# Part B of a two-part kernel: output of 32 tokens on four column tiles, the 8 look-ahead rows multiplied at the end

## Chip, cores and metric

One core of one Trainium2 chip. The metric is the device time of one execution in microseconds, the median of the runs (lower is better).

## What is computed

The output is two independent blocks joined along the last axis. Part A is a dilated sliding-window attention over 2048 tokens of width 640; the change leaves its instructions alone. Part B is a recurrent-memory transformer layer:

```
S, Dm, H, Dh, M, seg_len = 2048, 640, 32, 192, 8, 32          # 64 segments
mask = (idx[:, None] < M) | (idx[:, None] >= idx[None, :])     # over L = 40 tokens
for s in range(n_seg):
    h = concatenate([mem, x[32*s : 32*s+32]])                  # 8 memory + 32 tokens
    q, k, v = h @ Wq, h @ Wk, h @ Wv                           # each 40 x (32 heads x 192)
    p = softmax(where(mask, q k^T * Dh**-0.5, -1e9))
    o = (p v).reshape(40, 6144) @ Wo                           # 40 x 640
    mem = o[:8]                                                # goes into the next segment
    outs.append(o[8:])
```

All inputs and the output are bf16. The memory rows make the 64 segments a chain. Wq, Wk and Wv are 640 x 6144 and Wo is 6144 x 640, some 31 MB in all, which is more than fits on the core beside the rest.

## The kernel before, in words

**Weights.** Part B cuts each of Wq, Wk, Wv into 4 head groups g of 1536 columns and 5 pieces of 128 input rows (`dc`), and Wo into 24 units i of 256 rows. Such a unit is one [128, 1536] or [128, 1280] bf16 block (384 or 320 KB). Most stay on the core ("resident", tiles `wres_*`); 24 of them are fetched again in every segment through a ring of six buffers (`wstream`, tag `ws`, line 417, printed as `t<-wcopy_*`): 2 in each k group, 2, 2, 1 and 1 in the v groups, and the Wo units of `STREAMED["o"]`. SyncE issues these fetches in program order, and a fetch waits until TensorE has used the unit that was in its buffer six fetches before. Before Part B starts, the streamed units are copied into contiguous DRAM blocks (`wcopy_*`), and x is copied into one window per segment (`xwindows`, line 382).

**Tokens on the narrow side.** A projection (`project32`, line 485) takes 32 tokens as the stationary operand: four matmuls, one for each of TensorE's four 32-column tiles, each with 384 weight columns as the moving operand. A window holds two sets of 32 tokens. `main(s)` is the 8 memory rows and the first 24 tokens of segment s. `ahead(s)` is the last 8 tokens ("late rows") of four consecutive segments; these don't depend on the memory, so they are projected once for four segments (`RENEW`) and kept in buffers `Lb` (q, k) and `LV` (v). A DMA transpose (line 469) lays the window of the next segment out as [128 input rows, 5, 64].

**One segment**, the function `segment`, whose order on TensorE is written by hand: for each group g the projections of q, k, v; a turn of q and k by matmuls with the identity (line 498) into `QT` and `KT`; `scores` (line 575, 16 matmuls of 64 output rows); `softmax` and `put_p` on VectorE (lines 582 to 600) with the exponential on ScalarE (line 588); `turn_p` (lines 610 and 613); `mix` (line 627: 32 matmuls with 32 rows of weights and 40 columns on four row tiles, into four PSUM tiles, copied to `OT` by ScalarE and VectorE in turn, line 465). The groups are interleaved, so that TensorE works on another group while one is in its softmax. `project_out` (line 641) adds, over all 24 Wo units, the product of `OT` with Wo into one PSUM tile `Y` [128, 320]: 40 of 64 stationary columns are tokens, and two column tiles hold the two halves of the 640 output columns. For every segment it runs in six stretches, of 6, 4, 2, 4, 2 and 6 units.

**The boundary between segments.** When the last unit is in `Y`, ScalarE copies it to SBUF (line 708), TensorE turns the 8 memory rows with the identity (`memory_rows`, line 654, after four filler matmuls, line 648), and VectorE writes them into the next window `HX` (line 657). Only then can the next segment's first projection start. To have work at that point, TensorE projects one q group of late rows (`ql`) in two parts, three pieces ahead of the last Wo units and two behind.

**Engines.** The order on TensorE is fixed by hand; on the others a scheduler sets it. PSUM has 8 buffers of one bank in Part B: three `acc`, four `x` (turns, scores, mix) and one `y`. GpSimd copies kept late rows into `QT` and `KT` and issues the output DMAs.

Of the kernel before, what the change touches and what calls it, by code (L numbers as in the profile page):

```python
# [23 lines left out]
def part_a(ctx, tc, A_x, A_wqkv, A_wo, out, ident, emit_loads):  # L24
# [239 lines left out]
    with tc.manual_schedule(engines={mybir.EngineType.PE, mybir.EngineType.DVE, mybir.EngineType.Activation}):  # L264
# [4 lines left out]
        for b in range(-1, n_blk):  # L269
# [13 lines left out]
STREAMED = {"k": ((2, 4), (2, 4), (0, 4), (0, 4)), "v": ((0, 4), (0, 4), (2,), (2,)),  # L283
            "o": (3, 5, 7, 10, 11, 13, 17, 18, 22, 23)}
# [3 lines left out]
LEAD_IN, PAD = 114, 4  # L288
# [9 lines left out]
def part_b(ctx, tc, B_x, B_mem0, B_Wq, B_Wk, B_Wv, B_Wo, out, ident, n_seg, pre, nbuf, mid):  # L298
# [6 lines left out]
    w_in = {m: w.rearrange("(dc p) h e -> p dc (h e)", p=128) for m, w in (("q", B_Wq), ("k", B_Wk), ("v", B_Wv))}  # L305
    wo_v = B_Wo.rearrange("h e d -> (h e) d").rearrange("(i k p) d -> p i k d", p=128, k=2)

    def unit_src(u):  # L310
        m, c, dc = u
        if m == "o":
            return wo_v[:, c]
        return w_in[m][:, dc, 1536 * c:1536 * c + 1536]

    def unit_cols(u):
        return 1280 if u[0] == "o" else 1536

    copied = {}

    def copy_streamed():

        order = [(m, g) for m, g in need]
        units = []
        for m, g in order:
            if m == "o":
                units += [("o", i, 0) for i in range(6 * g, 6 * g + 6) if i in STREAMED["o"]]
            else:
                units += [(m, g, dc) for dc in range(5) if m != "q" and dc in STREAMED[m][g]]
        for u in units:  # L330
            copied[u] = dpool.tile([128, unit_cols(u)], BF16, name="wcopy_%s%d_%d" % u)[:]
            nc.sync.dma_start(unit_tile(copied[u], u), unit_src(u))
# [4 lines left out]
    for m, g in need:  # L337
        if m == "o":
            resident += [("o", i, 0) for i in range(6 * g, 6 * g + 6) if i not in STREAMED["o"]]
        else:  # L340
            resident += [(m, g, dc) for dc in range(5) if m == "q" or dc not in STREAMED[m][g]]
    res, wait = {}, set()

    def unit_tile(t, u):
        v = t[:, 0:unit_cols(u)]
        return v.rearrange("p (k d) -> p k d", k=2) if u[0] == "o" else v

    def place_resident(pool, units):
        for u in units:
            res[u] = pool.tile([128, unit_cols(u)], BF16, name="wres_%s%d_%d" % u)[:]  # L350

    def load_resident(units, engs):
        for k, u in enumerate(units):
            engs[k % len(engs)].dma_start(unit_tile(res[u], u), unit_src(u))
# [8 lines left out]
    XW = dpool.tile([n_seg, 2 * SEG, Dm], BF16, name="xwindows")  # L363

    def copy_windows():

        rows = [(XW[0, 0:M], mem2[0:M]), (XW[0, M:SEG], x2[0:SEG - M])]
        for a, b in ((1, 49), (49, n_seg)):
            rows.append((XW[a:b, 0:SEG], x2[SEG * a - M:SEG * b - M].rearrange("(s n) d -> s n d", n=SEG)))
        groups = x2.rearrange("(t n) d -> t n d", n=SEG)[:, SEG - M:SEG]  # L370
        groups = groups.rearrange("(m k) n d -> k m n d", k=4)
        windows = XW[:].rearrange("(m k) n d -> k m n d", k=4)
        for r in range(4):
            for i in range(4):
                dst = windows[r][:, SEG + M * i:SEG + M * i + M]
                if i >= r:
                    rows.append((dst, groups[i]))
                else:
                    rows.append((dst[0:n_seg // 4 - 1], groups[i][1:n_seg // 4]))
                    rows.append((dst[n_seg // 4 - 1], groups[i][n_seg // 4 - 1]))  # L380
        for dst, src in rows:
            nc.sync.dma_start(dst, src)

    def emit_loads(turn_x):
        turn_x(1)
        load_resident(resident[:n_pre], [nc.sync])
        turn_x(2)
        copy_streamed()
        return copy_windows
# [7 lines left out]
    HXs = [xpool.tile([128, 5, 64], BF16, name=f"HX{i}") for i in range(2)]  # L397
# [5 lines left out]
    qk_sb = pool("b_qk", bufs=3)  # L403
# [7 lines left out]
    wait.update(resident[n_pre + len(early):])  # L411
# [8 lines left out]
    def get_unit(u):  # L420
        if u in fetched:
            return fetched.pop(u)
        if u in res:
            if u in wait:
                wait.remove(u)
                load_resident([u], [nc.sync])
            return res[u]
        return fetch(u)
# [11 lines left out]
    KT = cpool.tile([128, 4, 4, L], BF16, name="KT")  # L440
# [3 lines left out]
    OT = cpool.tile([128, 12 * L + PADW], BF16, name="OT")  # L444
    free = [cpool.tile([128, 3, 4, M], BF16, name=f"Lb{i}") for i in range(BLOCKS)]
    late = {}
    VW = 448
# [3 lines left out]
    nc.gpsimd.memset(KT[:], 0.0)  # L451
    for t in [QT, OT]:
        nc.gpsimd.memset(t[:, t.shape[1] - PADW:], 0.0)
    for t in LV + [Vst]:
        nc.gpsimd.memset(t[:, 192:256], 0.0)

    copies = {"n": 0}
    S_, V_ = nc.scalar.copy, nc.vector.tensor_copy
    ENGINES = {"sb": {"q": (V_, S_, S_, S_), "k": (S_, S_, S_, S_)}, "late": (V_, V_, V_, V_),
               "QT": (S_, S_, S_, V_), "KT": (S_, S_, S_, S_), "V": (S_, V_, V_, S_), "LV": (V_, S_, S_, V_),  # L460
               "PT": (S_, V_, V_, V_)}

    def evacuate(dst, src):
        copies["n"] += 1
        (S_ if copies["n"] % 2 else V_)(dst, src)  # L465

    def load_x(s):
        if s < n_seg:
            nc.sync.dma_start_transpose(HXs[s % 2][:], XW[s])

    def main(s):
        return HXs[s % 2][:, :, 0:SEG]

    def ahead(s):
        return HXs[s % 2][:, :, SEG:2 * SEG]

    def project32(Xs, m, g, dcs=range(5), ps=None):
# [3 lines left out]
        for dc in dcs:  # L481
            w = get_unit((m, g, dc))
            for n, X in enumerate(Xs):
                for j in range(4):
                    nc.tensor.matmul(ps[n][32 * j:32 * j + 32, :], lhsT=X[:, dc, :],  # L485
                                     rhs=w[:, 384 * j:384 * j + 384],
                                     start=(dc == 0), stop=(dc == 4), tile_position=(0, 32 * j))
# [7 lines left out]
    def turn(sb, chunks=(0, 1, 2)):  # L495
        pt = ps_x.tile([128, len(chunks), 4, 32], FP32, tag="x", name="pt")
        for k, c in enumerate(chunks):
            nc.tensor.matmul(pt[:, k], lhsT=sb[:, 128 * c:128 * c + 128], rhs=ident, start=True, stop=True)  # L498
        return pt

    def tokens(t):
        return t[:, 0:12 * L].rearrange("p (j c n) -> p j c n", c=3, n=L)

    def fill(copy, m, n0, n1, src):

        if m == "q":
            copy(tokens(QT)[:, :, :, n0:n1].rearrange("p j c n -> p c j n"), src)  # L507
            return
        fill_outer(copy, n0, n1, src[:, 0:3:2])
        fill_middle(copy, n0, n1, src[:, 1])  # L510

    def fill_outer(copy, n0, n1, src):
        copy(KT[:, :, 0:3:2, n0:n1].rearrange("p j c n -> p c j n"), src)  # L513

    def fill_middle(copy, n0, n1, src):
        copy(KT[0:64, :, 1, n0:n1], src[0:64])
        copy(KT[64:128, :, 3, n0:n1], src[64:128])  # L517

    def turn_late(sb, m, g, s, start):

        pt = turn(sb)
        for t in range(start, next_start(m, g, start)):
            rows = pt[:, :, :, M * (t % 4):M * (t % 4) + M]
            if t == s:
                if m == "k" and g == 0:
                    fill_middle(V_, 32, L, rows[:, 1])
                    fill_outer(S_, 32, L, rows[:, 0:3:2])
                else:
                    fill(S_, m, 32, L, rows)
# [266 lines left out]
```

## Time and profile before

| what | us |
|---|---|
| median of three runs | 1973.57 |
| lowest and highest run | 1972.08, 1983.03 |
| span of the profiled execution, first to last instruction | 1976.8 |
| first projection of Part B | 171.1 |
| last Wo matmul starts after | 1969.9 |
| copies of the memory rows into HX, the first and the last | 218.36, 1943.46 |

The page gives no device time of the profiled execution beside its span. The profile has, for each engine, its busy time; a TensorE row's busy time is a union of overlapping matmuls. "DMA share" is the mean busy share of the core's 16 DMA engines. The chain of waits follows the work that ended last backwards: it names at each time what the program was waiting for. A releaser behind "<-" is what ended an idle time.

### The profile page before, as it was taken

To read this page: it belongs to the slowest core of one execution; us is meant where nothing else is said; L and a number is where in the kernel's file an instruction comes from. 1 tells how busy PE (TensorE), PEld (TensorE's weight loads), DVE (VectorE), ACT (ScalarE), POOL (GpSimd) and SP (SyncE) were. 2 spreads that over 40 slices of the span, in tenths; PEclk is the share of its full clock that TensorE was granted. 3 is DMA by queue.
4 is the path that set the end of the run, shared out by engine and by line. 5 is a ranking of instruction groups with operands and counts; after the bars stand their busy time and mean duration, and the time that the engine had idled before them with its cause. 6 is when DMAs were issued, how large, how long until landed. Compare 5 with 4: busy or idle time off the path is not lost.

```text
span 1976.8 us, 99618 instructions
## 1 busy us (share of the span) xinstructions
PE 1890.8 (96%) x43006; PEld 1221.6 (62%) x43006; DVE 1032.1 (52%) x3431; ACT 927.4 (47%) x2963; POOL 262.3 (13%) x1070
## 2 busy tenths in 40 slices
PE   8998899999999999999999999999999999999998
PEld 5665566666666666666666666666666666666665
DVE  4885454455444554455445554455445554555454
ACT  3554344444444454444444454444444444444443
POOL 2001011111111111111111111111111111111111
PEclk9999999999999999999999999999999999999999
DMA  9936999999999999999999999999999999999997
GB/s 332 298 111 227 341 324 312 327 326 326 324 321 324 322 328 315 329 319 331 326 318 322 329 330 314 325 315 316 327 328 324 327 327 315 338 325 329 315 328 262
DMA packets 278203, 621.62 MB, mean 314 GB/s; under 512 B 62089, under 2 KB 72329, under 8 KB 277449
## 3 DMA queue, kind: packets, MB, share of 16 engines
q1 hardware_dynamic: 272258, 609.17, 91.3%
q8 instruction: 337, 5.52, 1.1%
q0 software_dynamic: 5504, 6.07, 1.0%
q14 instruction: 104, 0.85, 0.1%
HBM read 602.01 MB, written 19.27 MB: 314 GB/s over the span
## 4 chain that ended last, share of the span: by engine, by line
PE 67%; DMA 17%; ACT 7%; DVE 6%; issue 2%; SPq 0%; ACTq 0%; POOL 0%; POOLq 0%; DVEq 0%
PE acc L485 31%; PE Y L641 17%; DMA t<-wcopy_k 7%; PE pt L498 7%; DMA t<-wcopy_o 6%; DMA t<-wcopy_v 4%; PE Sps L575 3%; PE pq L95 3%; PE OTps L627 3%; DVE prod L151 1%; ACT sb L712 1%; ACT OT L708 1%; PE pt L610 1%; ACT KT L513 1%; ACT t L588 1%
## 5 line engine op out<-in xcount | busy, mean ns | idle before, releaser
L485 PEld LDWEIGHTS <-HX 128*32 128x32 bf16 x19380 | 467.1, 96 | 283.8 <-issue 54.5
L641 PEld LDWEIGHTS <-OT 128*64 128x64 bf16 x6144 | 317.8, 110 | 137.0 <-ACT OT L465 25.0
L485 PE MATMUL acc<-t,HX 128*32 128x384 bf16 x4524 | 342.9, 328 | 19.0 <-DMA t<-wcopy_k 9.3
L641 PE MATMUL Y<-wres_o,OT 128*64 128x320 bf16 x3584 | 331.2, 302 | 9.9 <-DVE OT L465 5.1
L485 PE MATMUL acc<-wres_q,HX 128*32 128x384 bf16 x6460 | 333.6, 328 | 1.1 <-issue 0.7
L492 ACT CAST sb<-acc 128x384 bf16<-128x384 f32 x448 | 210.1, 478 | 152.0 <-PE acc L485 132.4
L641 PE MATMUL Y<-t,OT 128*64 128x320 bf16 x2560 | 266.7, 301 | 10.4 <-DMA t<-wcopy_o 8.8
L485 PE MATMUL acc<-wres_v,HX 128*32 128x384 bf16 x4520 | 251.7, 327 | 0.7 <-DMA wres_v<-in_B_Wv_dram 0.7
L485 PE MATMUL acc<-wres_k,HX 128*32 128x384 bf16 x3876 | 224.6, 327 | 0.3 <-DVE sb L492 0.3
L588 ACT ACTIVATE t<-t 128x160 f32<-128x160 f32 x256 | 86.4, 338 | 288.5 <-DVE t L587 284.5
L498 PE MATMUL pt<-ident,sb 128*128 128x128 bf16 x1938 | 182.4, 221 | 8.5 <-ACT KT L513 0.9
L582 DVE SCALAR_TENSOR_TENSOR t<-Sps,mask 128x160 f32<-128x160 f32 x256 | 82.9, 324 | 178.5 <-PE Sps L575 173.2
L465 ACT CAST OT<-OTps 128x120 bf16<-128x120 f32 x512 | 108.6, 266 | 140.4 <-PE OTps L627 139.2
L498 PEld LDWEIGHTS <-sb 128*128 128x128 bf16 x1938 | 109.4, 97 | 87.0 <-ACT sb L492 20.5
L590 DVE TENSOR_REDUCE sm<-t 128x4 f32<-128x160 f32 x256 | 82.0, 320 | 130.9 <-ACT t L588 130.9
L465 DVE CAST OT<-OTps 128x120 bf16<-128x120 f32 x512 | 123.7, 272 | 46.1 <-PE OTps L627 45.8
L513 ACT CAST KT<-pt 128x256 bf16<-128x256 f32 (+1 forms) x323 | 109.1, 343 | 78.6 <-PE pt L498 78.1
L517 POOL COPY KT<-Lb 64x32 bf16<-64x32 bf16 x189 | 40.0, 212 | 788.2 <-PE Sps L575 656.9
L575 PEld LDWEIGHTS <-QT 128*64 128x64 bf16 x4096 | 98.4, 112 | 59.1 <-issue 52.2
L575 PE MATMUL Sps<-KT,QT 128*64 128x40 bf16 x4096 | 113.9, 187 | 5.6 <-ACT QT L507 2.6
L657 DVE CAST HX<-pt 128x40 bf16<-128x40 f32 x63 | 12.6, 200 | 179.5 <-PE pt L654 179.5
L600 DVE TENSOR_TENSOR P<-t,sm 128x128 bf16<-128x128 f32 (+1 forms) x512 | 100.2, 237 | 11.2
(91 smaller groups left out, 2130.8 us busy)
## 6 DMA issues: line engine op xcount, KB each, us to landing
t<-wcopy_o SPq DMA_DIRECT2D x640, 320.0 KB, 4.9
t<-wcopy_k SPq DMA_DIRECT2D x512, 384.0 KB, 5.3
t<-wcopy_v SPq DMA_DIRECT2D x384, 384.0 KB, 5.3
wres_q<-in_B_Wq_dram SPq DMA_DIRECT2D x20, 384.0 KB, 7.8
wres_v<-in_B_Wv_dram SPq DMA_DIRECT2D x14, 384.0 KB, 7.9
wres_k<-in_B_Wk_dram SPq DMA_DIRECT2D x12, 384.0 KB, 7.8
wres_o<-in_B_Wo_dram SPq DMA_DIRECT2D x14, 320.0 KB, 7.1
wcopy_o<-in_B_Wo_dram SPq DMA_DIRECT2D x10, 320.0 KB, 9.6
```

The lines of the kernel that those rows point to most:

```text
L95: nc.tensor.matmul(pq[32 * d:32 * d + 32], lhsT=wcol[:, k, t, 4 * c + d, :], rhs=xTs[s][:, k, :], start=(k == 0), stop=(k == 4), tile_posi ...
L465: (S_ if copies["n"] % 2 else V_)(dst, src)
L485: nc.tensor.matmul(ps[n][32 * j:32 * j + 32, :], lhsT=X[:, dc, :], rhs=w[:, 384 * j:384 * j + 384], start=(dc == 0), stop=(dc == 4), tile_ ...
L492: copy(sb[:], p[:])
L498: nc.tensor.matmul(pt[:, k], lhsT=sb[:, 128 * c:128 * c + 128], rhs=ident, start=True, stop=True)
L513: copy(KT[:, :, 0:3:2, n0:n1].rearrange("p j c n -> p c j n"), src)
L575: nc.tensor.matmul(Sps[64 * g2:64 * g2 + 64, a, :], lhsT=QT[:, at:at + 64], rhs=KT[:, a, ((0, 1), (3, 2))[g2][part], :], start=(n == 0), s ...
L582: nc.vector.scalar_tensor_tensor(out=t1[:], in0=Sps[:], scalar=scale, in1=mask[:].unsqueeze(1).to_broadcast([128, 4, L]), op0=ALU.mult, op ...
L588: nc.scalar.activation(t1[:], t1[:], ACTF.Exp)
L590: nc.vector.tensor_reduce(out=sm[:], in_=t1[:], axis=AX.X, op=ALU.add)
L600: nc.vector.tensor_tensor(out=P[:, k, :, at:at + hi - lo], in0=t1[:, :, lo:hi], in1=sm[:].unsqueeze(2).to_broadcast([128, 4, hi - lo]), op ...
L641: nc.tensor.matmul(Y[64 * gv:64 * gv + 64, :], lhsT=OT[:, L * c:L * c + 64], rhs=w[:, n:n + 320], start=(i == 0 and r == 0), stop=(i == 23 ...
```

## The change

The diff rewrites much of Part B. It does this:

- **Output of 32 tokens.** `project_out` takes only the 32 `main` tokens: four matmuls per Wo unit (2 row halves r x 2 column halves gv), each on a 32-column tile of its own. Even and odd halves are added afterwards: `close` has ScalarE copy the odd half (2 copies of 64 x 160), VectorE add it to the even half (2 adds), transpose the sum in 32 x 32 blocks and copy 8 columns of each block into the next window.
- **Late rows at the end.** The mixed late rows of each segment are copied by GpSimd into a tile `OL` and written to DRAM (`late_o`, 96 KB per segment). After the last segment `project_late` reads them back (16 DMAs of 384 KB) and multiplies 512 rows by all of Wo, in two passes over the 24 units.
- **x turned by VectorE.** The window is loaded by a plain DMA (`XS`) and transposed in 32 x 32 blocks by VectorE (`turn_x`, in `segment` after `mix(2)`). For that the rows of Wq, Wk and Wv are regrouped, and the window copies in DRAM are cut into four parts of 160 columns (100 or so DMAs in place of 26).
- **Mix on 64-row tiles.** A mask `own` blanks foreign heads, so that `mix` is 16 matmuls with 64 rows and 80 columns, into two PSUM tiles; the copy of the turned P becomes a VectorE multiplication of 128 x 320 for every group.
- **Scores** work on a new layout of `QT` and `KT`: 8 matmuls with 64 rows and 8 with 128.
- **One engine for each PSUM tile**: all copies of one tile are on one engine, and `QT`/`KT` are filled by one copy. `memory_rows` and its fillers are gone; `ql` is split two and three; `tq` and `tk` turns stand at other places.

```diff
+    XW = dpool.tile([n_seg, 4, SEG, 2, 160], BF16, name="xwindows")
+    late_o = dpool.tile([n_seg, 128, 48 * M], BF16, name="late_o")
...
+    def load_x(s):
+        if s < n_seg:
+            nc.sync.dma_start(XS[:], XW[s].rearrange("j n w c -> (j n) (w c)"))
+    def turn_x(s):
+        if s < n_seg:
+            nc.vector.transpose(HXs[s % 2][:].rearrange("p w k n -> p (w k n)"), XS[:])
...
     def scores(g):
-        for n in range(8):
-            a, part = n // 2, n % 2
-            for g2 in range(2):
-                at = L * (3 * a + g2 + part)
-                nc.tensor.matmul(Sps[64 * g2:64 * g2 + 64, a, :], lhsT=QT[:, at:at + 64], ...
+        for outer in range(2):
+            for a in range(4):
+                for h in range(2):
+                    k0, k1, c = (0, 128, 2 * h) if outer else (64 * h, 64 * h + 64, 1)
+                    at = L * (4 * c + a)
+                    nc.tensor.matmul(Sps[64 * h:64 * h + 64, a, :], lhsT=QT[k0:k1, at:at + 64], ...
+                                     tile_position=(k0, 64 * h))
...
     def turn_p(g):
-        ENGINES["PT"][g](PT[:], pt[:].rearrange("p l (h n) -> p l h n", h=2)[:, :, :, 0:L])
+        nc.vector.tensor_tensor(PT[:], pt...to_broadcast([128, 4, 2, L]), own[:]...to_broadcast([128, 4, 2, L]), op=ALU.mult)
     def mix(g, PT):
+        plan = [(late, h, 0) for late in range(2) for h in range(2)] + [(late, h, 1) for late in range(2) for h in range(2)]
+        for n, (late, h, middle) in enumerate(plan):
+            k, col, lo, hi = (1, 128 + 64 * h, 64 * h, 64 * h + 64) if middle else (2 * h, 256 * h, 0, 128)
+            for r in range(2):
+                nc.tensor.matmul(ps[r][lo:hi, 2 * L * k:2 * L * k + 2 * L], lhsT=V[64 * r:64 * r + 64, col:col + hi - lo], ...
+        for r, copy in ((0, S_), (1, V_)):
+            copy(OT[:, 6 * r:6 * r + 6].rearrange("p c n -> p (c n)"), ps[r][:, 0:6 * L])
+        nc.gpsimd.tensor_copy(OL[:, :, 12 * g:12 * g + 12].rearrange("p n c -> p c n"), OT[:, :, 32:L])
...
     def project_out(Y, g, pairs=range(6)):
-                    nc.tensor.matmul(Y[64 * gv:64 * gv + 64, :], lhsT=OT[:, L * c:L * c + 64],
-                                     rhs=w[:, n:n + 320], ..., tile_position=(0, 64 * gv))
+                    t = 32 * (2 * r + gv)
+                    nc.tensor.matmul(Y[t:t + 32].rearrange("p (b c) -> p b c", b=2),
+                                     lhsT=OT[:, slot(c), 0:32], rhs=wide(w, r, gv),
+                                     start=(i == 0), stop=(i == 23), tile_position=(0, t))
+    def close(s, Y):
+        for b in range(2):
+            S_(odd[64 * b:64 * b + 64], Y[64:128, 160 * b:160 * b + 160])
+        for b in range(2):
+            nc.vector.tensor_tensor(Ysb[64 * b:64 * b + 64], Y[0:64, 160 * b:160 * b + 160],
+                                    odd[64 * b:64 * b + 64], op=ALU.add)
+        if s + 1 < n_seg:
+            nc.vector.transpose(T, Ysb)
+            nc.vector.tensor_copy(HXs[(s + 1) % 2][:, 0, :, 0:M], T.rearrange("p (k n) -> p k n", n=SEG)[:, :, 0:M])
+        for j in range(4):
+            nc.gpsimd.dma_start(out2[SEG * s:SEG * s + SEG - M, Dm + 160 * j:Dm + 160 * j + 160], Ysb[32 * j + M:32 * j + SEG])
+        nc.gpsimd.dma_start(late_o[s], OL[:].rearrange("p n c -> p (n c)"))
...
     def segment(s):
         mix(2, PT[2])
+        turn_x(s + 1)
         values(s, 3)
...
-            ql = project32([ahead(s + 1)], "q", gl, range(0, 3))
+            ql = project32([ahead(s + 1)], "q", gl, slice(0, 2))
         project_out(Y, 3)
-        nc.scalar.copy(Ysb, Y[:])
+        close(s, Y)
         if not last:
-            project32([ahead(s + 1)], "q", gl, range(3, 5), ql)
+            project32([ahead(s + 1)], "q", gl, slice(2, 5), ql)
             nc.scalar.copy(sb[:], ql[0][:])
-            memory_rows(s, Ysb)
-            turn_late(sb, "q", gl, s, s + 1)
+            turn_late(sb, "q", gl, s, s + 1, V_)()
+    def project_late():
+        for b in range(16):
+            nc.sync.dma_start(t, late_o[4 * b:4 * b + 4].rearrange("i p c -> p i c"))
+        for part in ((0, 1, 2), (3,)):
+            for i in range(24):
+                w = get_unit(("o", i, 0))
+                for r in range(2):
+                    for m in part:
+                        for gv in range(2):
+                            for j in range(4):
+                                nc.tensor.matmul(sums[2 * m + gv][32 * j:32 * j + 32, 0:320], lhsT=O[4 * m + j][:, :, at],
+                                                 rhs=w[:, 640 * r + 320 * gv:640 * r + 320 * gv + 320], ...)
+            for m in part:
+                ...  # two copies to SBUF, then 16 DMAs of 8 rows to the output, on SP and ACT in turn
```

349 lines of the change are left out of this document (179 added, 170 removed).

## The prediction

> **What bounds the kernel now.** I read the page first, then windows of a few microseconds, the waits of TensorE, the chain of waits through two segments, and the instruction orders of both programs.
>
> ```profile
> span 1976.8 us, 99618 instructions
> PE 1890.8 (96%) x43006; PEld 1221.6 (62%) x43006; DVE 1032.1 (52%) x3431; ACT 927.4 (47%) x2963; POOL 262.3 (13%) x1070
> q1 hardware_dynamic: 272258, 609.17, 91.3%
> ```
>
> TensorE is busy 96% of the span, but the DMA queue is at 91.3%: two resources are near their limits together. Windows tell how near the second one is:
>
> ```profile
> core 0: us, PE busy (x) PEld busy (x) DVE busy (x) ACT busy (x) POOL busy (x), PEclk, DMA share, GB/s
> 40.00:45.00 5.00, 5.00 (x92) 3.16 (x85) 4.20 (x5) 2.69 (x5) 0.00 (x0) 1.00 1.04 403
> 246.00:1943.00 1697.00, 1643.54 (x38938) 1063.46 (x38932) 863.60 (x3142) 802.63 (x2655) 231.21 (x976) 1.00 0.96 324
> ```
>
> With a deep queue of weight loads the DMA engines moved 403 GB/s; in Part B they move 324 at a share of 0.96. So the share overstates the load, and there is room for some 20% more. TensorE's waits for streamed units in this stretch are 8.6 + 6.8 + 5.9 = 21.3 us, 0.34 us in each of 62 segments.
>
> The copies of the memory rows stand at 218.36 and 1943.46, so a segment takes 1725.1 / 62 = 27.82 us. The chain through one segment without DMA waits (27.1 us), where a number behind x counts matmuls:
>
> ```profile
> 1027.80 2.55 PE acc L485 x60
> ...
> 1030.79 0.93 PE acc L485 x20
> 1031.72 0.02 issue
> 1031.74 0.43 PE Sps L575 x16
> ...
> 1037.73 0.31 PE OTps L627 x32
> ...
> 1039.52 1.75 PE Y L641 x24
> 1041.27 0.24 PE Sps L575 x16
> ...
> 1050.61 0.35 issue
> ...
> 1051.78 1.77 PE Y L641 x24
> 1053.55 0.03 ACTq L708
> 1053.58 0.04 issue
> 1053.62 0.43 ACT OT L708
> 1054.05 0.47 ACT sb L712
> 1054.51 0.05 issue
> 1054.56 0.34 PE pt L498 x3
> 1054.90 2.55 PE acc L485 x60
> ```
>
> It is TensorE nearly throughout. Sixty projection matmuls take 2.55 and twenty 0.93: 0.81 for twenty, so 0.162 for a set of four on four tiles, and 0.12 to enter. Scores take 0.43 behind a projection (32-column tiles) and 0.24 behind the output (64-column tiles, as their own): another form of tile costs 0.1 to 0.2.
>
> **Per segment, part by part.**
>
> *Output.* Now 96 matmuls at 1.75/24: 7.0. Afterwards 24 sets of four with 320 columns in place of 384: 0.162 x 320/384 = 0.135, so 3.25, and an entry of 0.12 in four of the six stretches (two now follow a projection and keep its form): 3.7. **-3.3**. That four tiles run side by side is what the projections show.
>
> *Boundary.* Now 1.35 from the end of Y (1053.55) to the next projection (1054.90). Afterwards ScalarE makes two copies of 64 x 160; its 64 x 128 copy takes 0.26 and its 128 x 320 one 0.43, so 0.29 each. Then come `sb` 0.47, hop 0.05, the turn 0.34, and VectorE's first copy of a late block (`Lb`, 0.26): in the built order it stands between the transpose and the copy into HX (0.2 in the old row), so the memory rows wait behind a turn that they don't need. With 0.07 and two short hops: 2.0. VectorE's own part (first add after 0.36, two adds at 0.35, a transpose) ends at 1.3 to 1.5 and is hidden by the turn. No row here has a VectorE transpose; its bounds are the 128 x 32 copy (0.17) and the 128 x 384 one (0.55), and for the 128 x 320 transpose of x I take 0.42, near the 128 x 320 copy. +0.65, less 0.16 for the third `ql` piece that now lies inside: **+0.5**. The output DMAs and `late_o` are on GpSimd (five at 0.5) ahead of its fills of QT and KT, which are needed only some 4 us into the segment: nothing.
>
> *Mix.* 32 matmuls of 40 columns take 0.31. Afterwards there are eight steps of 80 columns and, inside, a change from 64 x 128 to 64 x 64 tiles: at least 0.31, at most 0.5; I take 0.42, in the middle, since halves can overlap. **+0.45** for four (0 to +0.75).
>
> *Scores and turns.* The two score runs behind the output lose their cheap entry (0.2 and 0.1), each run changes its form inside (0 to 0.12; I take 0.05), and turns that stood in runs of six now stand alone (six in 0.44, three in 0.27: 0.1 twice): **+0.7**.
>
> [...]
>
> *Group 3.* From its scores to P takes 2.6 (three VectorE steps 0.32 to 0.35, exponential 0.34, sum 0.32, reciprocal 0.17, two products 0.47, one OT copy between). TensorE's cover is two Wo units, mix, v, four units: now 3.0 or so, afterwards 0.37 + 0.42 + 0.93 + 0.54 = 2.3. It waits 0.3 (not where v3 is renewed). Behind P, VectorE has the x transpose (0.42) and the wider PT (320 elements: 0.55 for 384, 0.33 for 160, so 0.49 in place of 0.33) before `mix(3)` may start; TensorE has two units: 0.4 of waiting, in place of the 0.35 at 1050.61 (not in each segment). **+0.4**.
>
> *Group 1.* PT of group 0 moves from ScalarE into VectorE's chain (0.49), and the built order puts an OT copy (0.41) ahead of the P products in three of four segments: P(1) is ready 6.3 after the first scores, TensorE at 5.7, unless a renewed k or v fills it. 0.6 in half of the segments: **+0.3**.
>
> *Waits for DMA.* Per segment 8.78 MB of units, and 0.2 of windows, late rows and output: 9.0 MB in 27 us is 333 GB/s. Against that, a window's DMA now holds SyncE 0.3 and not 1.2. I take +0.1, between -0.3 and +0.5.
>
> Sum: -3.3 + 0.5 + 0.45 + 0.7 + 0.4 + 0.3 + 0.1 = **-0.85**, a period of 27.0. VectorE's load rises from 13.7 to some 17 us, still two thirds. 63 segments: **-54 us**. The first one is bound by loads and stays.
>
> **The end.** From the last Y to the end now: 1970.6 to 1976.8, 6.2. Afterwards the first row of `project_late` needs twelve blocks of late rows; SyncE reaches eight of them only behind the last fetches, some 4.6 before the end of Y, and at 1.0 to 1.1 each (0.384 MB) they are in at +8. Pass one is 24 x 2 x 3 x 2 = 288 sets of four: 39. Pass two is 96 sets: 13, and 3 of waiting, since SyncE issues 24 output DMAs (0.3 to 0.5 each) ahead of its last fetches. Two copies, eight DMAs per queue and a landing: 7. Together 70, less 6.2 and rounding: **+65** (55 to 95).
>
> **The start.** SyncE issues 26 window DMAs from 92.84 to 116.17, 0.62 apart where nothing holds it; it then has slack to 146.9. Afterwards there are 104 with more, shorter rows: 104 x 0.62 = 64, and some 4 more in each part for the two long ones (estimate from the 2.5 of the first transpose with its thousands of rows): 173, and 3.5 for landing and turning, against 171.1: **+5** (0 to +35).
>
> 1976.8 - 54 + 65 + 5 = 1992.8. The span is 3.2 above the median of the runs: **1990**. Break-even is a period of 27.82 - 70/63 = 26.7.
>
> **Rivals.**
>
> *The waits don't come (faster).* Form changes cost nothing inside scores and mix (-0.9), and TensorE's early arrivals at P(3), mix(3) and P(1) are covered, since other stalls are gone with the single copies and the two free `x` buffers (-0.5): a period of 25.6, 1976.8 - 140 + 70 - 3 = 1904. It decides from 26.7 down. For it: ScalarE and VectorE copies in turn on one tile held each other up (VectorE 72.5 us, ScalarE 52.6 us behind each other's Lb copies). Against: the form change is seen in the rows, the VectorE order in the built program. 0.33.
>
> *DMA is the bound.* Its queue moved 609.17 MB in 91.3% of 1976.8: 337 GB/s while busy, and 9.0 MB at that rate is 26.7, to which the boundary's idle adds: 27.6. 1976.8 - 14 + 70 - 3 = 2030. Against: 403 GB/s with a deep queue. 0.13.
>
> *Start and end dearer.* [...] 0.09.
>
> *The four tiles don't overlap*, the output stays at 7: 27.82 + 2.5, and the late pass doubles: 2250. The projections speak against it. 0.03.
>
> My forecast, a period of 26.7 to 27.3 (1970 to 2010): 0.42.
>
> **Chances.** Runs of this kernel differ by about 0.5%, 9.9 us: 1963.7 to 1983.4 is the same. The forecast gives 0.11 same and 0.31 slower; the first rival 0.32 faster and 0.01 same; the forecast's lower edge adds 0.01 to faster, the others are slower. Faster 0.33, same 0.12, slower 0.55. The range 1920 to 2050 leaves out the fastest tenth (a period under 25.8) and the last rival.
>
> **What would show it.** Y sets at 0.135; 2.0 us between Y and the next projection, ending in HX behind an Lb copy; TensorE waiting at P(3) and mix(3) for PT; 65 to 70 us behind the last segment. A period under 26.7 makes it wrong; so does a DMA rate that stays at 324 while TensorE waits for `t`.

## The result, and the profile after

The changed kernel takes 2098.18 us (median of four runs, 2095.58 to 2111.01) against 1978.24 for the old one beside it: 1.062 times as long (95% interval 1.058 to 1.066). The forecast was 1990 with a range of 1920 to 2050. It was wrong. Here and below a time is the median of a kernel's executions, without those more than 1.5% above its fastest (two, of the kernel with half of the output, at a clock of 0.94 against 0.96 in its fastest).

The page of the changed kernel, in the same three lines as before:

```profile
span 2096.8 us, 92560 instructions
PE 1845.2 (88%) x39688; PEld 1105.1 (53%) x39688; DVE 1127.7 (54%) x3463; ACT 808.6 (39%) x2100; POOL 466.8 (22%) x1138
q1 hardware_dynamic: 287812, 622.35, 88.3%
```

TensorE is busy for 46 us less, in a span that is 120 us longer. The copies of the memory rows into HX (line 675) place these 120 us. The first one stands at 262.06 (before 218.36), the last at 1991.50 (before 1943.46). So the start costs +43.7; 62 periods of 27.89 in place of 27.82 cost +4.3; and what follows the last copy takes 105.3 in place of 33.3, +72.0.

Windows of the changed kernel: the loading of resident weights, the stretch behind it, and the middle of Part B (columns: busy time and instructions of each engine, then granted clock, DMA share, GB/s):

```profile
20.00:60.00 40.00, 37.34 (x596) 23.79 (x588) 29.79 (x31) 21.31 (x41) 0.00 (x0) 1.00 1.04 218
60.00:86.00 26.00, 0.01 (x3) 0.00 (x0) 0.00 (x0) 0.43 (x1) 0.00 (x0) 0.60 1.08 233
300.00:1850.00 1550.00, 1400.96 (x31285) 818.78 (x31285) 869.94 (x2895) 627.01 (x1669) 387.61 (x945) 0.99 0.94 326
```

The old kernel's window from 20 to 60 us:

```profile
20.00:60.00 40.00, 37.45 (x612) 24.55 (x604) 30.53 (x31) 21.62 (x40) 0.00 (x0) 1.00 1.09 368
```

From 20 to 60 us DMA now moves 218 GB/s, where it moved 368. From 60 to 86 us TensorE stands still, for the third transposed block of Part A's x lands behind these loads (one wait of 26.9 us). In Part B TensorE is busy 1401 of 1550 us (before 1502), and DMA moves 326 GB/s, as before.

The chain through a segment of the changed kernel:

```profile
1065.96 5.46 DMA t<-wcopy_o
...
1071.46 0.34 PE Y L660 x4
...
1071.87 0.29 ACT odd L668
...
1072.17 0.30 ACT odd L668
...
1072.90 0.33 DVE OT L670
...
1073.25 0.35 DVE T L674
1073.59 0.14 DVE Lb L551
1073.73 0.09 DVE HX L675
...
1073.87 1.81 PE acc L521 x40
...
1078.08 0.47 PE px L588 x16
...
1084.20 0.45 PE px L636 x16
...
1086.14 0.93 PE Y L660 x24
...
1087.28 6.66 DMA t<-wcopy_o
```

Fetches of units stand in the chain for 5 to 7 us at a time: the walk goes from TensorE to the fetch it waits for, and then to the earlier use that freed the fetch's buffer. They are not new, but they have grown: from 300 to 1940 us they are 28.0% of the chain (Wo 21.0, k 5.2, v 1.8), where the old kernel has 16.9% (Wo 6.3, k 6.9, v 3.7). New is the boundary: from the last Y (end 1071.80) to the projection (1073.87) it is ScalarE's two copies, VectorE's adds, transpose and two copies, 2.07 us in all.

### The profile page after: what moved, and what is told of

Its sections match the earlier page's. It is cut to its first block, busy times and chain, and to the rows that moved or that the text cites. A ratio compares the mean times of both kernels' runs of the same rounds, so it can differ in the third digit from the quotient of the medians.

```text
span 2096.8 us, 92560 instructions
## 1 busy us (share of the span) xinstructions
PE 1845.2 (88%) x39688; PEld 1105.1 (53%) x39688; DVE 1127.7 (54%) x3463; ACT 808.6 (39%) x2100; POOL 466.8 (22%) x1138
## 4 chain that ended last, share of the span: by engine, by line
PE 53%; DMA 31%; DVE 5%; SPq 4%; ACT 3%; issue 3%; ACTq 0%; DVEq 0%; POOLq 0%; POOL 0%
PE acc L521 29%; DMA t<-wcopy_o 19%; PE Y L660 6%; PE px L534 6%; DMA t<-wcopy_k 5%; PE px L588 4%; SPq L409 4%; PE px L636 3%; ACT odd L668 2%; DMA t<-wcopy_v 1%; PE px L756 1%; DVE OT L670 1%; DMA wres_k<-in_B_Wk_dram 1%; DMA wres_v<-in_B_Wv_dram 1%; DMA wres_q<-in_B_Wq_dram 1%
## 5 line engine op out<-in xcount | busy, mean ns | idle before, releaser
L642 POOL COPY OL<-OT 128x96 bf16<-128x96 bf16 x256 | 165.8, 648 | 598.1 <-DVE OT L641 368.5
L534 PE MATMUL px<-ident,sb 128*128 128x128 bf16 x1938 | 204.3, 223 | 55.0 <-ACT sb L733 46.9
L660 PE MATMUL Y<-t,OT 128*32 128x320 bf16 x2560 | 189.9, 306 | 46.3 <-DMA t<-wcopy_o 40.5
L660 PEld LDWEIGHTS <-OT 128*32 128x32 bf16 x6144 | 145.6, 96 | 144.5 <-issue 65.0
L660 PE MATMUL Y<-wres_o,OT 128*32 128x320 bf16 x3584 | 211.5, 306 | 1.0 <-DMA wres_o<-in_B_Wo_dram 0.9
L579 ACT CAST Vst<-acc 128x384 bf16<-128x384 f32 x256 | 122.7, 479 | 153.4 <-PE acc L521 151.7
L623 DVE TENSOR_TENSOR PT<-px,own 128x320 bf16<-128x320 f32 x256 | 124.2, 485 | 65.4 <-PE px L620 61.6
L588 PEld LDWEIGHTS <-QT 64*64 64x64 bf16 (+1 forms) x4096 | 105.1, 108 | 86.8 <-issue 77.0
L677 POOL DMA_DIRECT2D out_dram<-OT x256 | 128.2, 507 | 84.0 <-DVE OT L670 77.9
L588 PE MATMUL px<-KT,QT 64*64 64x40 bf16 (+1 forms) x4096 | 138.0, 189 | 3.8 <-issue 0.7
```

The lines of the kernel that those rows point to most:

```text
L534: nc.tensor.matmul(pt[:, c], lhsT=sb[:, 128 * c:128 * c + 128], rhs=ident, start=True, stop=True)
L579: copy(t[:], p[:])
L588: nc.tensor.matmul(Sps[64 * h:64 * h + 64, a, :], lhsT=QT[k0:k1, at:at + 64], rhs=KT[k0:k1, c, a, :], start=(outer == 0 and a == 0), stop= ...
L623: nc.vector.tensor_tensor(PT[:], pt.rearrange("p l (h n) -> p (l h) n", h=2)[:, :, 0:L].unsqueeze(2) .to_broadcast([128, 4, 2, L]), own[:] ...
L642: nc.gpsimd.tensor_copy(OL[:, :, 12 * g:12 * g + 12].rearrange("p n c -> p c n"), OT[:, :, 32:L])
L660: nc.tensor.matmul(Y[t:t + 32].rearrange("p (b c) -> p b c", b=2), lhsT=OT[:, slot(c), 0:32], rhs=wide(w, r, gv), start=(i == 0), stop=(i ...
```

## The experiments

The old kernel ran beside every group, at 1973 to 1978 us. Periods are means over 62 copies into HX of one profiled execution each. Five kernels below differ from the changed one only in how the resident weights are loaded ahead of the loop; their periods run from 27.70 to 28.04, so a difference of less than some 0.3 between two periods shows little by itself.

**What holds the period.** *Less work for TensorE.* Half the moving columns in 22 of the 24 Wo units:

```diff
-  rhs=wide(w, r, gv)
+  rhs=wide(w, r, gv)[:, 0:nb]          # nb = 1 for 22 of the 24 units
```

> The changed kernel with half of the output product left out (160 of 320 moving columns in 22 of the 24 Wo units): 44 sets shorter by 0.068, so TensorE has 3.0 less 1.5 us of output work per segment, while all fetches stay. Theory one (TensorE sets the period): 27.87 less 1.5 is 26.4, 2098 becomes 2006. Theory two (six buffers and the transfers set the period, so that time taken from TensorE comes back as waits for units): the period stays above 27.3, over 2062. Between them the share that comes back is read off.

(The saving is 22 sets of 0.068, 1.5 us; the "44" and the "3.0" in the text are slips.) Measured: 2103 and 2130 us, a period of 27.91 in the first. TensorE lost some 1.4 us of work per segment (its output rows fall from 4.26 to 2.91) and the period did not move. Its waits from 300 to 1900 us (columns: total, times, longest), first one row of the changed kernel, then two of this run:

```profile
PE Y L660 <- DMA t<-wcopy_o: 34.8, 60, 2.1
PE Y L661 <- DMA t<-wcopy_o: 52.6, 89, 2.3
PE px L588 <- ACT KT L539: 14.8, 53, 0.3
```

By the period this is theory two, but not all of it is waiting for units. Of the idle time that came back, 0.9 us per segment, waits for Wo units have a third (34.8 to 52.6 us). The rest are waits for copies by other engines (for `KT` 14.8 us, for P and PT another 19). And other rows of TensorE lasted longer; the granted clock fell from 0.99 to 0.97. So this run alone does not show that the ring holds the period; the next ones do.

*Fewer transfers.* The ten streamed Wo units are not fetched:

```diff
+  if u[0] == "o": return res[("o", 0, 0)]
   return fetch(u)
```

> The changed kernel without the fetches of the ten streamed Wo units: these products read another unit that stays on the core, so this part of the output is not the reference's. TensorE's work is the same, DMA moves 5.5 MB per segment in place of 8.8. Theory one (TensorE and its hand-overs set the period; waits for units are what the trace shows, 0.92 us per segment): the period falls from 27.87 to 26.9 to 27.0, and the end, with no fetches in its second pass, by some 3: 2098 becomes about 2037. Theory two (the fetches also slow the rest: SyncE, GpSimd's DMAs, the clock): below 26.5, under 2010. Theory three (it is not the transfers): over 2085.

1984 us, a period of 26.49: theory two by the time, and just so by the period. The trace shows 0.9 us of waits for units per segment, but the transfers cost 1.4.

*Bandwidth or depth.* Eight buffers with all bytes; and half the bytes with six buffers:

```diff
-  nbuf=6
+  nbuf=8                               # two resident k units left out
```

> The changed kernel with eight buffers in the ring of streamed units in place of six; the room comes from two resident k units that are left out (their products read a neighbour, so that part is not the reference's). Every fetch stays, with its bytes. Theory one (bandwidth: the engines can't move more than the 326 GB/s that all these kernels show): the period stays at 27.7 to 27.9, and the time at 2085 to 2098. Theory two (depth: with six buffers a fetch is issued too late, and the queue runs thin; with 403 GB/s seen in the old kernel's preload there is bandwidth to spare): the period falls to 26.5 to 26.9, near the 26.49 of the kernel without Wo fetches: 2012 to 2037.

2011 us, a period of 26.56, and no wait for a unit in its view of waits. Its middle window:

```profile
300.00:1850.00 1550.00, 1437.66 (x32892) 848.84 (x32888) 908.73 (x3045) 658.91 (x1755) 410.70 (x999) 1.00 0.97 343
```

Theory two: with the same fetches the engines moved 343 GB/s. So 326 was no limit of bandwidth; six buffers were.

```diff
-  nc.sync.dma_start(t[:, 0:unit_cols(u)], copied[u])
+  nc.sync.dma_start(t[:, 0:n], copied[u][:, 0:n])       # n = half of the columns
```

> The changed kernel with half of each streamed unit fetched (the products use the fetched half twice, so their output is not the reference's): the same 24 fetches per segment in the same order and ring, the same TensorE work, 4.4 MB in place of 8.8. Theory one (bandwidth): as without the Wo fetches, a period of 26.4 to 26.5, and with shorter loads of the first units and at the end 1975 to 2005. Theory two (depth, where the fixed part of a fetch, its issue and its latency of some 2.5 us, weighs as much as its bytes): a period of 26.8 to 27.4, 2025 to 2065.

1984 us, a period of 26.44: theory one's number. It does not contradict the run before: with half the bytes, 177 GB/s at a share of 0.61, a ring of six left no wait for a unit in the view of waits either. I read the two together so: what counts is the whole landing time, bytes and queue included, against the time between a use and the sixth use after it. That the depth counts is measured; this reading of why is not.

*Was the old kernel held too?* The same two edits to it:

> The kernel before, without the fetches of its ten streamed Wo units (their products read a resident unit; the output is not the reference's). Its trace shows 0.34 us of waits for units per segment. Theory one (the old kernel was bound by TensorE, as its 96% say): the period falls by at most these waits, 27.82 to 27.5, and the time to 1954. Theory two (it already stood at the limit of the transfers, which show as small stalls everywhere): the period falls by 0.6 or more, under 1937. In either case the gap to the changed kernel's 26.49 without Wo fetches is what the change took from TensorE and the hand-overs: 1.0 by theory one, less by theory two.

> The kernel before with eight buffers in its ring in place of six, the room taken from two resident k units (left out; their products read a neighbour). Theory one (the old kernel too was held by the depth of the ring): its period falls from 27.82 to the 26.96 that it has without Wo fetches, or within 0.1 of it: 1918 to 1930. Theory two (only the changed kernel, with its shorter output stretches, runs into the ring; what the old one loses to transfers is bandwidth): at most the 0.34 us of visible waits go, 1950 or more.

Without Wo fetches 1920 us and a period of 26.96: 0.86 less, not the 0.34 of visible waits; theory two. With eight buffers 1950 us, 27.46, by both numbers theory two of that run: 0.36 of the 0.86 comes back. Of the 0.50 that stays, some 0.3 is idle time without a releaser, the last section's subject; the rest are rows of TensorE that last longer. That bandwidth takes it, as this theory has it, is not shown.

*Seven buffers with a 25th fetch*, all of the computation kept, on both kernels:

```diff
-  nbuf=6      "k": (2, 2, 2, 2)        # old kernel: "k": ((2, 4), ...)
+  nbuf=7      "k": (3, 2, 2, 2)        # old kernel: "k": ((0, 2, 4), ...); changed one: another order in k group 0
```

> The changed kernel with seven buffers and a ninth streamed k unit (25 fetches), all of the computation kept. Depth: between 27.87 with six and 26.56 with eight, and a little more data: a period of 26.9 to 27.3, 2038 to 2062. Bytes: 28.3 or more, over 2120.

> The kernel before with seven buffers, all of the computation kept: the room comes from a ninth k unit that is streamed (the first of group 0), so 25 fetches and 9.2 MB per segment in place of 24 and 8.8. If depth is what counts, a seventh buffer gives more than the extra 0.39 MB takes: a period of 27.0 to 27.3, 1925 to 1945. If bytes count, the period rises to 28.2 or more, over 1995.

The changed kernel: 2035 us, a period of 26.82, somewhat better than expected, though it moves more data (354 GB/s). The old one: 1974.4 against 1977.5 (95% interval of the ratio 0.996 to 1.002), a period of 27.68, so neither theory. No version here that keeps the whole computation is clearly faster than the old kernel.

*The spacing of the uses.* Two other choices of streamed units on the old kernel:

> The kernel before with another choice of the 24 streamed units, everything else the same (six buffers, the same bytes, all of the computation kept). With the times at which TensorE uses each unit in the run without Wo fetches, the choice was made so that a use and the sixth use after it lie as far apart as possible: three of k group 0, two of k1, one each of k2 and k3, 2, 1, 2 and 2 of v, and Wo units 0, 3, 5, 8, 10, 14, 16, 18, 22, 23. Theory one (what holds the ring is the spacing of uses six apart): the period falls by 0.2 to 0.4, 1950 to 1963. Theory two (only the number of buffers or bytes matters, or the old choice is as good): 27.7 to 27.9, 1968 to 1978.

> The kernel before with seven buffers and 25 streamed units, as in the run with seven buffers (1974), but these chosen in the same way for uses seven apart (three of k0, two each of k1 and k2, one of k3, 2, 2, 2 and 1 of v, Wo units 1, 5, 6, 9, 11, 12, 17, 18, 19, 23). Theory one (spacing): the remaining waits for units, 10.8 us in all in the run with seven buffers, go: 27.4 to 27.5, 1955 to 1963. Theory two (with a deeper queue something else holds TensorE, as its idle time without a releaser grew from 7.6 to 11.6 us): 27.6 to 27.8, 1968 to 1980.

Both lost: 2012 us (28.34) and 1994 us (28.14). In the first, waits for k units at the segment's start rose to 42.8 us from 300 to 1850 us. So theory one fell in the form in which I had worked it out: uses six apart, taken from a run without stalls, don't predict the period. Whether spacing counts in another form stays open. In the second, theory two held: only 3.3 us of waits for k units were left, yet TensorE's unexplained idle time grew (last section).

**The start.** *One DMA per unit over 128 rows* in place of four of 32 rows per block:

```diff
-  for j in (0, 2, 1, 3):
-      dma_start(t[32*j:32*j+32]..., w_in[m][j, :, dc:dc+n, ...])
+  for i, (_, _, d) in enumerate(units):
+      dma_start(t[:, 1536*i:1536*i+1536], w_in[m][:, :, d, ...])
```

> The changed kernel with one edit: the resident weights are loaded by one DMA per unit over all 128 rows of the tile, not by four DMAs of 32 rows each per block. In the changed kernel the DMA engines moved 216 to 222 GB/s between 20 and 60 us at a share of 1.03, where the old kernel moved 392 to 399, and TensorE stood still from 60 to 86 us for the third transposed block of x. Theory (the narrow DMAs are slow: 3072-byte packets at 231 ns in place of 126): the rate goes back to about 398 GB/s, the stall of 26 us in Part A goes, SyncE begins the window copies at 93 in place of 119 and ends at 172 in place of 198, and the first copy of the memory rows falls from 262 to 236 to 243: 2098 becomes 2072 to 2079. Rival (the regrouped rows of Wq, Wk and Wv are slow to read, whatever the tile side looks like): the rate stays near 220 and the time at 2098.

2191 us, much slower, and not by either theory: 102 GB/s at a DMA share of 0.26, first copy at 361. Packets lasted 121 ns (median), as in the old kernel's loads (125), but the engines were busy for a quarter of the time. The regrouped source has 4 as its outermost dimension; the same DMAs from plain rows (below) had a share of 1.05 and 374 GB/s. So the layout of the source makes the difference; how it does so is not shown.

*Two queues*, row groups 0 and 2 on SyncE, 1 and 3 on GpSimd; then 0 and 1 against 2 and 3:

```diff
-  nc.sync.dma_start(...)
+  (nc.sync, nc.gpsimd)[j % 2].dma_start(...)        # second run: [j // 2]
```

> The changed kernel with one edit: of the four 32-row DMAs that load a block of resident weights, two are issued by SyncE (row groups 0 and 2) and two by GpSimd (groups 1 and 3), so that two row groups are written at the same time. Theory one (what makes a packet last 231 ns in place of 121 is that all 16 engines write the same 32 rows of SBUF at once): packets get shorter and the rate rises from 220 to between 300 and 400 GB/s from 20 to 60 us, the stall of 26 us in Part A shrinks by 13 to 26, and the time falls to 2072 to 2085. Theory two (the DRAM side of the regrouped rows is slow): packets stay at 231 ns, the rate at 220, and the time at 2098 or, with GpSimd's issues, above.

> The changed kernel; of the four 32-row DMAs of a block SyncE issues those of row groups 0 and 1, GpSimd those of groups 2 and 3, so that rows below and above 64 are written at the same time (the run with two queues had paired 0 with 1 and 2 with 3 in time). [...] Theory two (the DRAM side of the regrouped rows, or the engines serve one transfer after the other): 220 GB/s, 2098 to 2112. [...]

2112 and 2108 us. In the second, packets on SyncE's queue fell from 233 to 181 ns (medians from 20 to 60 us), the rate there was 247 GB/s in place of 218, and the time gained nothing. TensorE's standstill only moved: it was busy 17 of the 40 us from 20 to 60, and worked from 60 to 86.

*Which side is slow?* Plain neighbouring rows of DRAM, once with 128-row DMAs, once with 32-row DMAs (weights in another order than x):

```diff
+  w = B_W.rearrange("(dc p) h e -> p dc (h e)", p=128)
+  dma_start(t[:, 1536*i:1536*i+1536], w[:, d, ...])              # 128 rows
+  dma_start(t[32*j:32*j+32]..., w[32*j:32*j+32, dc:dc+n, ...])   # 32 rows
```

> The changed kernel with the resident weights of q, k and v loaded as in the old kernel: one DMA per unit, 128 rows, from 128 neighbouring rows of DRAM (so these weights are in another order than x, and the output of Part B is not the reference's). Both theories of the slow loading: 390 to 400 GB/s from 20 to 60 us, no stall in Part A; SyncE's window copies then run from 93 to 172, and the first copy of the memory rows falls from 262 to 236 to 243: 2072 to 2079. If the stall stays, the loading is not its cause.

> As in the run with plain 128-row loads (weights in another order), but with the changed kernel's shape on the tile side: four DMAs of 32 rows per block. Theory one (the 32 rows of SBUF make it slow): packets of 220 to 235 ns, 216 to 222 GB/s, the stall of 26 us in Part A, 2098. Theory two (the regrouped rows of DRAM make it slow): 121 to 127 ns, some 400 GB/s, 2072 to 2079.

Their windows from 20 to 60 us, with 128 rows:

```profile
20.00:60.00 40.00, 35.69 (x572) 22.40 (x564) 29.49 (x30) 21.01 (x39) 0.00 (x0) 1.00 1.05 374
```

and with 32:

```profile
20.00:60.00 40.00, 37.34 (x600) 25.11 (x594) 30.13 (x31) 21.60 (x40) 0.00 (x0) 1.00 1.04 223
```

The same DRAM rows, 374 against 223 GB/s, packets of 122 against 232 ns (medians): the shape on the side of SBUF, 32 rows in place of 128, is the cause. With 128 rows the stall in Part A is gone, the first copy stands at 224.4 and the time is 2066; with 32 rows the copy is at 262.1 and the time 2093. Why 32 rows take longer is not shown; with row groups 0 and 1 written beside 2 and 3 the rate was 13% higher (247 against 218 GB/s) and the time no shorter (2108).

*The window copies* in their old layout:

```diff
-  XW = [n_seg, 4, SEG, 2, 160]     # 104 copies, one load per window
+  XW = [n_seg, SEG, 2, Dm]         # 26 copies, four loads per window
```

> The changed kernel with one edit: the windows of x in DRAM have their old layout (26 copies in place of 104), and each window is then loaded by four DMAs of 32 rows in place of one. Theory (104 issues on SyncE, 79 us from 119 to 198, hold back the first weight fetches): the copies end at about 143, behind Part A's stall nothing waits for them, Part B starts 10 to 13 us earlier, and the first copy of the memory rows falls from 262 to about 250: 2098 becomes 2085 to 2088, less what three more DMAs per segment on SyncE cost (0 to 0.3 us per segment, 0 to 19 in all). Rival (the start is set by the 32-row loads and the clock alone): first copy at 262, 2098 or more.

2092 us (2084 to 2108, against 2096 to 2111). The first copy fell by 12.3 to 249.8, as the theory said. Little of it is left in the time: the period was 0.18 longer, which lies within the spread named above, or is the price of three more DMAs per segment.

**The end.** Late rows neither written nor multiplied:

> The changed kernel without the late rows' way out: no writes of mixed late rows to DRAM (96 KB per segment) and no multiplication of them at the end, so the last 8 tokens of each segment's output are missing. The tail from the last Y to the end should fall from 79 to about 6: 2098 becomes 2025. Theory one (the writes cost nothing): the period stays at 27.87, 2025. Theory two (the transfers bind, so 0.1 of 9.1 MB counts): the period falls by 0.1 to 0.3, 2006 to 2019.

2027 us: what follows the last copy falls from 105.3 to 32.8, and the period stays at 27.90. Theory one: the end is dear, and no cost of the writes to DRAM is seen; a tenth or two per segment would not show in one period.

**The boundary.** With eight buffers, the Lb copies by ScalarE:

```diff
-  turn_late(sb, "q", gl, s, s + 1, V_)()
+  turn_late(sb, "q", gl, s, s + 1, S_)()
```

> The changed kernel with eight buffers (two k units left out, as before: 2011 us, period 26.56), and at the boundary the copies of the kept late rows (Lb) made by ScalarE, so that VectorE goes from the transpose straight to the copy into HX. The trace of the changed kernel has 0.14 for the Lb copy between them. Theory one (it is on the path, now that transfers don't hold the period): 0.1 to 0.2 less per segment, 26.36 to 26.46, 1999 to 2005. Theory two (the turn of the late rows ends as late anyway): 26.5 to 26.6, 2008 to 2014.

2004 us against 2011 (ranges 2002 to 2008 and 2004 to 2014), but a period of 26.57 against 26.56: theory two for the period. From the first odd copy to the start of HX it is 1.75 in place of 1.79: the Lb copy's 0.14 mostly overlapped its neighbours.

## Why the prediction was wrong

**Where the time is.** The forecast's span was 1992.8, the measured one 2096.8. Of the 104 us between them the loop has 58 (forecast -54, measured +4), the start 39 (+5 and +44) and the end 7 (+65 and +72). Three terms failed: "+0.1" for waits for DMA, which left out what a ring of six costs; the sum of TensorE's parts, which saved less than half of what was forecast; and "+5" for the start, which left out the 32-row loads. Neither the loop nor the start alone takes the time out of the range; the two together do.

**The load of the transfers.** The step that failed is the way from "so the share overstates the load, and there is room for some 20% more" to the term "+0.1". The room is there, as 403 GB/s in a preload and 343 with eight buffers show. But a fetch can be issued only when the sixth use before it is over, so a fetch can come late while the engines have room, and no average rate shows it. The output that went from 7.1 to 3.9 us per segment is just where ten of the 24 uses stand. The old profile had a sign: fetches are 17% of its chain, but the chain that the prediction worked from was one segment without them. The visible waits were taken for the whole cost, too: 0.34 us where the run without Wo fetches gave 0.86. Of these 0.86, 0.48 are idle time of TensorE and 0.38 are busy rows that last longer (26.96 against 26.58 us per segment); why they do is not shown.

Free of the limit (old: without Wo fetches; changed: eight buffers) the periods are 26.96 and 26.56, so the limit costs 0.86 and 1.34 per segment. Of the 1.34, at most 0.3 are the clock, whose mean was 0.99 and with eight buffers 1.00. The change made this item +0.48, for a forecast of +0.1; with the spread of the periods this is good to some 0.2. The split depends on what is compared: with no Wo fetches on both sides it is +0.54, and -0.47 for TensorE's parts; with eight buffers on both sides it is +0.98 and -0.90, but there the old kernel still loses 0.50 to the fetches. The sign that the prediction named came true: the rate stayed at 326 while TensorE waited for `t`.

**TensorE's parts**, from the old kernel without Wo fetches and the changed one with eight buffers, each matmul counted from where the one before it ends (us per segment):

| part | forecast | measured |
|---|---|---|
| output | -3.3 | 7.07 to 3.93: -3.14 |
| boundary | +0.5 | waits for `sb` and HX 1.27; memory rows, fillers and a wait gone, 0.58: +0.69 |
| mix | +0.45 | 1.24 to 1.86: +0.62 |
| scores and turns | +0.7 | 1.35 to 1.93 and 2.50 to 2.71: +0.79 |
| groups 3 and 1 | +0.7 | waits +0.33, turns of P 0.58 to 0.75: +0.50 |
| rest | 0 | +0.14 |
| sum | -0.95 | -0.40 |

The signs are right, but the saving is a little smaller than forecast and all added costs but one are larger, and that adds up: 0.55 per segment, 34 us in all, where the transfers missed by 0.38, 24 us. A set of the output starts every 0.136, as forecast (0.135). A change of form inside scores or mix costs 0.08 to 0.09 beside the usual step (0.112 and 0.128 between matmuls that otherwise follow at 0.03 to 0.04). So each of these changes had its price in the trace, and the two items came to +1.41 where I had +1.15. VectorE's transpose of x, taken as 0.42, lasts 0.50. The boundary is 2.07 for a forecast of 2.0, but for another reason: I had the turn and the Lb copies on the path and VectorE hidden. The first add waits for both odd copies, so VectorE's adds and transpose end last, and moving the Lb copies gave nothing in the period. That the total is near the forecast is luck.

**The start** (+5, measured +43.7) was mis-sized because a part of the diff was not costed: the four 32-row DMAs per block. That is the larger part (the first copy falls by 37.7 with 128-row DMAs of plain rows). The 104 window copies, which I did cost, give 12.3 by themselves (the two overlap, so they don't add up); they lasted from 119 to 198 us, 79 in all, near the 80 that their terms sum to, but began 26 us late.

**The end** (+65, range 55 to 95) was right: from the last Y, which ends at about 2018, to 2096.8 it is 79 in place of 6, +72. Its late rows come 10 us after that (forecast 8), pass one takes 40 (39), pass two 22 (13 and 3), copies and output 6 (7). The excess is mostly in pass two, in this chain:

```profile
2068.55 0.58 ACTq L767
...
2073.82 1.24 DMA out_dram<-wres_q
2075.09 2.99 DMA t<-wcopy_o
2078.11 3.16 DMA out_dram<-wres_q
2081.28 0.28 SPq L767
2081.66 0.35 SPq L447
2082.12 3.25 DMA t<-wcopy_o
2085.40 0.37 PE acc L756 x4
```

and in this window of pass two:

```profile
2068.24:2090.57 22.33, 17.05 (x392) 15.91 (x384) 0.97 (x3) 0.81 (x3) 0.00 (x0) 0.85 0.37 110
```

SyncE's last fetches stand behind output DMAs, as the prediction said. TensorE waits for them twice, 5.1 us in all and not 3. After each wait the granted clock is 0.50 for 3.4 us, where a set takes 0.27 and not 0.136; that is another 3. In the run without Wo fetches pass two takes 13.3.

**The rivals.** "DMA is the bound" had a period of 27.6, near the measured 27.89, and that is luck: it put the limit at 337 GB/s, and with seven and eight buffers the same engines moved 354 and 343 in a shorter period. What it had right is that the transfers keep the period up. "Start and end dearer" came true by its signs: of the start's 44 us the 104 window copies gave 12. No run shows that stationary columns 96 bytes apart, as in the late pass, slow a set: at a clock of 1.00 it took 0.136 there, as in the loop. I had treated the two rivals as alternatives. The faster rival needed TensorE to set the period; even at 26.56, 62 periods save 78 us against the old kernel, and start and end cost 116.

## What to carry to other kernels

Here an average rate (326 GB/s) and the sum of visible waits (0.34 us per segment in the old kernel) showed neither the limit that the ring of buffers set nor what the fetches cost (0.86 there, and 1.34 in the changed kernel with its shorter output stretches). Varying the depth showed it: in the changed kernel six, seven and eight buffers gave periods of 27.89, 26.82 and 26.56. Comparing the landing time of a fetch with the time from a use to the use one ring later is a way to think of it, but choices of units made by that measure were slower. Before costing what a change does in the loop, cost every DMA whose shape it alters: how many rows of SBUF it covers (32 in place of 128: 223 against 374 GB/s here) and how its source is laid out (regrouped in place of plain rows: 102 against 374). Work moved out of a loop to the end must be paid out of what the loop truly saves, and two rivals that don't exclude each other need a case in which both come true.

## What the runs showed of the hardware that I had not expected

- In the loads from 20 to 60 us a 3072-byte packet into SBUF lasted 121 to 125 ns (medians) where the DMA covered 128 rows, and 232 to 233 where it covered 32. With plain rows the DMA share was 1.05 and 1.04, so here it did not tell the slow transfer from the fast one.
- With units that arrived in time another wait appeared. In the old kernel TensorE sometimes idles inside `mix` (32 short matmuls) without a releaser. In the waits from 300 to 1850 us, the old kernel with seven buffers and the other choice of units has

```profile
PE OTps L627 <- issue: 27.8, 34, 2.1
```

  and with eight buffers

```profile
PE OTps L629 <- issue: 11.0, 21, 1.5
```

  Over the same stretch it is 4.6 us in the unedited kernel and 0.2 without Wo fetches. In the kernels that show it such an idle time ends 1.4 us (medians 1.39 to 1.45) after the last 16 KB packet of the instruction queue had ended, so TensorE probably waits for its instructions, which the old kernel's page lists as a DMA queue (`q8 instruction`, 337 packets, 5.52 MB); no run separated this. It is part of why eight buffers gave the old kernel only 0.36 of the 0.86.
- The granted clock fell where TensorE waited more: 1.00 in the old kernel's middle stretch, 0.99 in the changed one's, 0.97 with half of the output left out. In the changed kernel's middle stretch it fell to 0.50 for 3.4 or 6.8 us at a time; nine such times make the 0.99. More waiting alone was not enough: the changed kernel with eight buffers is idle for 7% of that stretch, more than the old one (3%), at 1.00.
